# Scores of the first segment from unpermuted weights, and a list scheduler that may hold an engine free

## The chip, the cores and the metric

The kernel runs on one core of a Trainium2 chip. The metric is the device time of that core in microseconds (us); lower is better. Before the change it was 562.31 us, the median of three runs (559.48 to 563.02).

The engines are named as the profile names them: PE (TensorE matmuls), PEld (its weight loads), DVE (VectorE), ACT (ScalarE), POOL (GpSimd), SP (the queue that issues DMAs). "The granted clock" is the share of full TensorE clock that the trace shows; 1.00 is full speed.

## The reference, cut to what matters

Two passes over the same four sublayers: A, B, A, B, each behind a layer norm and with a residual. There are 2048 tokens, 512 channels, 32 heads of 16, all in bf16.

```python
# A: 4 segments of 512 tokens; causal softmax inside a segment, a compressive memory across them
for s in range(4):
    p = softmax(qs @ ks.T * 0.25 + causal_mask)         # per head, 512 x 512
    o = g * (phi(qs) @ M) / (phi(qs) @ z) + (1 - g) * (p @ vs)
    M, z = M + phi(ks).T @ vs, z + phi(ks).sum()
x = x + concat(o) @ wo
# B: linear attention with softmax feature maps
phi_q = concat(softmax(q @ w_phi), softmax(-(q @ w_phi)));  phi_k likewise
o = phi_q @ (phi_k.T @ v) / (phi_q @ phi_k.sum())
x = x + o @ wo_B
```

The work of a pass falls into A's four segments with their score exponentials (40 exponentials of 128x1024 elements for a segment, 160 for a pass), then B's queries and the change to the next pass.

## The kernel before

The program is a graph of operations. Each states the engines that could run it with an assumed duration for each, what it reads and what it writes. A list scheduler, which runs in Python when the kernel is built, simulates this graph and so chooses each engine's order and the buffers; the program then runs in that fixed order on every engine, with semaphores for what crosses engines. So an engine that waits for one operation does not run the next.

The heart of the scheduler takes, for each engine that is free, the most urgent operation that is ready:

```python
def forward(self, prio, pools):
    ...
        for e in ENGS:
            if free[e] > now + 1e-9 or not ready[e]:
                continue
            ...
            while ready[e]:
                pr, i = heapq.heappop(ready[e])
                o = ops[i]
                ...
                if e == "dve" and o.port and free["pool"] > now + 1e-9:
                    held = True          # DVE op that shares a port with POOL: not while POOL is busy
                elif can_alloc(o):       # its buffers are to be had
                    pick = o
                    break
                skipped.append((pr, i))
...
def schedule(self, pools, rounds, off):
    ...
    for r in range(rounds):              # ROUNDS = 5
        mk = self.forward(prio, pools)
        if best is None or mk < best[0]:
            best = (mk, list(prio))
        fin = [o.end for o in self.ops]
        prio = self.backward(fin)
```

In sublayer A, a score matmul takes four heads at once. The keys of eight heads lie in one 128-row tile, two half tiles of 64 rows; the queries are spread to `Q4`, where slot `s` holds only the rows of every fourth head, the rest zero. For this the weights of K and Q are first permuted within each 64 columns, so that the head index is the fastest:

```python
for g in range(NG):
    for k in ("k", "q"):
        for hf in range(2):
            ...                                      # 16 operations, "perm"
            self.g.op({"act": (520, ... activation(dst(), src(), ACT.Copy)),
                       "dve": (285, ... tensor_copy(dst(), src()))},
                      [self.WAraw[k][g // 2]], [R("WP", k, g, hf)], label="perm", port=True)
```

Segments after the first fill `Q4` by DMA into zeroed buffers. The first one, segment (0, 0), has no time for that and writes four whole slots by a multiply with a mask per partition, on ACT or DVE:

```python
self.wproj(ps, 0, self.WA["q"], [R("WP", "q", g, h) for h in range(2)], g, xT, ..., label="Q")
self.evac(lambda: QT.t[:], lambda: ps.t[:, 0:512], 512, [ps[0]], [QT], label="Qev")
for sl in range(nd, 4):                              # nd = 0 in segment (0, 0)
    m = self.S4[:, sl:sl + 1]
    self.g.op({"dve": (262, ... tensor_scalar(Q4.t[:, sl, :], QT.t[:], m, None, op0=ALU.mult)),
               "act": (566, ... activation(Q4.t[:, sl, :], QT.t[:], ACT.Identity, scale=m))},
              [QT, R("S4")], [Q4[sl]], label="Qm", port=True)
...
# the scores of query tile i against key tile j; waits for ALL of Q4
self.mm(... KT.t[:, hf, j*128:(j+1)*128], Q4.t[:, :, i*128:(i+1)*128] ...,
        [512] * 2, [KT[0], KT[1], (Q4, ALLKEYS)], [S], opens=[PT], label="S")
self.act(lambda: PT.t[:], lambda: S.t[:], ACT.Exp, 1024, [S], [PT], scale=0.25, label="exp")
```

There are six `Q4` buffers. Two are zero-filled at the start, after a gate on the normalisation of the fourth token tile:

```python
self.pQ.init[i] = self.g.op({"pool": (1800.0, ... memset(tq[:], 0.0)),
                             "dve": (1070.0, ... memset(tq[:], 0.0))}, [], [], label="zero")
...
gate = self.xnop[3]
for o in ... + list(self.pQ.init.values()):
    o.deps.add(gate)
```

The softmax here doesn't subtract the row's maximum and nothing guards it: scores larger than these inputs give would overflow.

Of the kernel before, what the change touches and what calls it, by code (L numbers as in the profile page):

```python
# [8 lines left out]
ACT = mybir.ActivationFunctionType  # L9
# [11 lines left out]
NG = 4  # L21
# [65 lines left out]

LAT = {"pe": 190, "act": 160, "dve": 130, "pool": 100, "sp": 60}


class Graph:
# [39 lines left out]
    def op(self, ch, reads=(), writes=(), opens=(), kind="c", lat=None, label="", ndma=0, port=False):  # L131
        o = Op()
        o.id = len(self.ops)
        o.ch = ch
        o.deps = set()
        o.succ = []
        o.tiles = []
        o.opens = list(opens)
        o.kind = kind
        o.lat = lat  # L140
        o.label = label
        o.ndma = ndma
        o.need = False
        o.port = port
        o.vc = None
        for r in reads:
            self._touch(o, r, False)
        for w in writes:
            self._touch(o, w, True)
        o.deps.discard(o)  # L150
        self.ops.append(o)
        return o
# [65 lines left out]
    def forward(self, prio, pools):  # L218
        ops = self.ops
        n = len(ops)  # L220
        left = [len(o.deps) for o in ops]
# [26 lines left out]
        now = 0.0  # L248

# [22 lines left out]
        while len(order) < n:  # L272
# [25 lines left out]
# [3 lines that stand above are left out]
                skipped = []  # L301
                pick = None
                held = False
# [3 lines that stand above are left out]
                    if o.eng is not None:  # L307
                        continue
                    if e == "dve" and o.port and free["pool"] > now + 1e-9:
                        held = True  # L310
                    elif can_alloc(o):
                        pick = o
                        break
                    skipped.append((pr, i))
                for x in skipped:
                    heapq.heappush(ready[e], x)
                if pick is None:
                    if held:
                        wake.append(free["pool"])
                    continue  # L320
                o = pick
                for t in o.opens + o.tiles:
                    if t.slot is None:
                        pl = t.pool
                        t.slot = pl.free.pop(0)
                        t.base = pl.base[t.slot]
                        pl.live[t.cls] = pl.live.get(t.cls, 0) + 1
                        pl.opened[t.cls] = pl.opened.get(t.cls, 0) + 1
                o.eng = e
                o.seq = len(order)  # L330
                o.start = now
                dur = o.ch[e][0]
                o.end = now + dur
                free[e] = o.end
                order.append(o)
                lt = o.lat if o.lat is not None else LAT[e]
                heapq.heappush(ev, (o.end + lt, 1, o.id))
                heapq.heappush(ev, (o.end, 2, o.id)) if False else None
                for s in o.succ:
                    left[s.id] -= 1  # L340
                    l2 = 0 if (e == "pe" and "pe" in s.ch and o.kind == "c") else lt
                    rt[s.id] = max(rt[s.id], o.end + l2)
                    if left[s.id] == 0:
                        heapq.heappush(ev, (rt[s.id], 0, s.id))
            nxt = [free[e] for e in ENGS if ready[e] and free[e] > now + 1e-9] + wake
# [11 lines left out]
    def schedule(self, pools, rounds, off):  # L357
        self.link()
        self.log = []
        prio = [float(o.id) for o in self.ops]  # L360
        best = None
        for r in range(rounds):
            try:
                mk = self.forward(prio, pools)
            except RuntimeError as ex:
                if r == 0:
                    raise
                print("round", r, str(ex)[:1200])
                break
            self.log.append(round(mk / 1000, 1))  # L370
            if best is None or mk < best[0]:
                best = (mk, list(prio))
            fin = [o.end for o in self.ops]
            prio = self.backward(fin)
            prio = [p + off.get(o.label, 0.0) for p, o in zip(prio, self.ops)]
        self.model_us = self.forward(best[1], pools) / 1000.0
# [111 lines left out]
class Kernel:  # L488
# [20 lines left out]
    def mm(self, items, cols, reads, writes, opens=(), label=""):  # L509

        dur = sum(max(c / 2.4, 25.0) + 0.5 for c in cols)

        def fn(e):
            ins = None
            for out_ap, lhsT, rhs, st, sp in items():
                ins = e.matmul(out_ap, lhsT, rhs, start=st, stop=sp, tile_position=(basep(lhsT), basep(out_ap)))  # L516
            return ins
        return self.g.op({"pe": (dur, fn)}, reads, writes, opens, label=label)
# [23 lines left out]
    def tpe(self, out_ap, src, reads, writes, opens=(), label=""):  # L542

        ps = self.T(self.pG, "gen")
        pb = lambda: ps.t[:, :].bitcast(BF16)[:, 0:512]

        def fn(e):
            for k in range(4):
                ins = e.transpose(pb()[:, k * 128:(k + 1) * 128], src()[:, k * 128:(k + 1) * 128], self.ident[:])
            return ins  # L550
        self.g.op({"pe": (240.0, fn)}, list(reads) + [self.R("ident")], [ps], opens=opens, label=label + "p")
        self.evac(out_ap, lambda: pb().rearrange("p (a b) -> p a b", a=4), 512, [ps], writes, label=label + "e", fast=True)
# [65 lines left out]
    def setup(self):  # L618
# [4 lines left out]
        def load(pairs, kb, writes, eng="sp", opens=()):  # L623
            dur = 780.0 if eng == "pool" else 470.0
            o = self.g.op({eng: (dur, lambda e: [e.dma_start(o, i) for o, i in pairs()])}, [], writes, opens, kind="d",
                          lat=1300.0 + kb / 0.25, label="load", ndma=1)
# [19 lines left out]
        load(lambda: [(self.beta_sb[:], inp["A_beta"].partition_broadcast(128))], 8, [R("beta")], "pool")  # L646
        self.early = len(self.loads)
# [5 lines left out]
        load(lambda: [(self.wphi_st[:], inp["B_w_phi"].rearrange("(g hl) d j -> (hl d) g j", g=NG))], 16, [R("wphi")])  # L653
# [4 lines left out]
        for g in range(NG):  # L658
# [9 lines left out]
          150, [R("H8")], [R("H8")], eng=P)  # L668
        A8w = self.T(self.pS, "set")
# [7 lines left out]
        v(lambda e: e.tensor_tensor(self.S4[:], self.A8[:, 0:4], self.A8[:, 4:8], ALU.add), 70, [R("A8")], [R("S4")])  # L677
# [13 lines left out]
          [R("gt"), R("A8")], [R("GAm")])  # L691
        v(lambda e: e.tensor_copy(self.GAm[:, :, :, 16], self.A8[:, None, :].to_broadcast([128, NG, 8])), 100,
          [R("A8")], [R("GAm")])
# [29 lines left out]
    def fold_weights(self):  # L723
# [12 lines left out]
        for k in ("k", "q"):  # L736
            raw = self.WBraw[k]
            W = self.T(self.pX, "raw")
            for dt in range(4):
                self.tr(lambda W=W, dt=dt: W.t[:, :, dt * 128:(dt + 1) * 128], lambda raw=raw, dt=dt: raw.t[:, dt, :], [raw], [W[dt]], label="foldT")  # L740
# [72 lines left out]

    def a_proj(self, L, s):
# [5 lines left out]
        for g in range(NG):  # L820
# [5 lines left out]
            self.wproj(ps, 0, self.WA["k"], [R("WP", "k", g, h) for h in range(2)], g, xT, opens=[KT] + ([pk] if pk else []), label="K")  # L826
# [4 lines left out]
            if pk:  # L831
                PK = self.T(self.p1, "PhK")
                self.phi(ps, pk)
                self.tr(lambda PK=PK: PK.t[:].rearrange("p (a b) -> p a b", a=4), lambda pk=pk: pk.t[:], [pk], [PK], label="PhKtr")
# [5 lines left out]
            self.wproj(ps, 0, self.WA["q"], [R("WP", "q", g, h) for h in range(2)], g, xT, opens=[QT] + ([PQ] if PQ else []), label="Q")  # L840
            self.evac(lambda QT=QT: QT.t[:], lambda ps=ps: ps.t[:, 0:512], 512, [ps[0]], [QT], label="Qev")
            nd = 0 if (L, s) in MASKED else 4
            if nd:
                for a in range(0, nd, 2):
                    fn = lambda e, Q4=Q4, QT=QT, a=a: [e.dma_start(Q4.t[sl::4, sl, :], QT.t[sl::4, :]) for sl in (a, a + 1)]
                    self.g.op({"sp": (1300.0, fn)}, [QT], [Q4[("d", a)]], kind="d", lat=1650.0, label="Qx", ndma=2)
            for sl in range(nd, 4):
                m = self.S4[:, sl:sl + 1]
                self.g.op({"dve": (262, lambda e, Q4=Q4, QT=QT, sl=sl, m=m: e.tensor_scalar(Q4.t[:, sl, :], QT.t[:], m, None, op0=ALU.mult)),
                           "act": (566, lambda e, Q4=Q4, QT=QT, sl=sl, m=m: e.activation(Q4.t[:, sl, :], QT.t[:], ACT.Identity, scale=m))},  # L850
                          [QT, R("S4")], [Q4[sl]], label="Qm", port=True)
# [26 lines left out]
    def a_att(self, L, s, i):  # L878
# [9 lines left out]
        for hp in range(2):  # L888
            PV = self.T(self.pG, "pv")
            pvv = lambda PV=PV: PV.t[:, 0:288].rearrange("p (h c) -> p h c", c=18)  # L890
            for gg in range(2):
# [3 lines left out]
                for j in range(i + 1):  # L895
# [5 lines left out]
                        [512] * 2, [KT[0], KT[1], (Q4, ALLKEYS)], [S], opens=[PT], label="S")  # L901
# [209 lines left out]
    def build(self):  # L1111
# [9 lines left out]
        for L in range(2):  # L1121
            if L == 0:
                lnA(0, 0)
                gate = self.xnop[3]
                for o in self.loads[self.early:self.second] + [self.pK.init[k] for k in range(3, 6)] + list(self.pQ.init.values()):
                    o.deps.add(gate)
                self.a_proj(0, 0)
                self.fold_weights()
            for s in range(NSEG):
# [10 lines left out]
                for i in range(4):  # L1140
                    self.a_att(L, s, i)
                    self.ln(s * 4 + i, self.xB[(L, s)], pe=("xB", L, s * 4 + i) in PE_T)
                self.b_keys(L, s, TOK[s])
# [24 lines left out]
ROUNDS = 5  # L1168
OFF = {"warm": 1e6}
N_WARM = 14  # L1170

# [36 lines left out]
```

## Time and profile before

| | before |
|---|---|
| median of 3 runs | 562.31 us |
| profiled span, mean granted clock | 559.1 us, 0.984 |
| first projection / first 1024-wide exp | 11.4 / 20.9 us |
| 20th / 120th / 160th exp | 57.4 / 183.2 / 227.8 us |
| from the 160th exp to the end | 331.3 us |

The exponentials are a good clock for this kernel: the first 160 of them on ACT, 128x1024 each, are exactly the scores of the first pass. I read their start times from the timeline of each trace (to about 0.1 us, because its rows merge operations).

The page of the kernel before: busy times, the span in 40 slices (tenths of busy; the row PEclk is the granted clock), and the share of the engines in the chain of waits that ended last.

```profile
PE 518.8 (93%) x5548; PEld 287.6 (51%) x5548; DVE 450.3 (81%) x992; ACT 495.3 (89%) x652; POOL 220.4 (39%) x395
...
PE   8769899999999999998989998999999899999896
...
PEclk9999999999999999997998999999999999999799
...
PE 53%; DVE 21%; ACT 17%; DMA 4%; POOL 2%; issue 1%; SPq 1%; DVEq 0%
```

No engine limits alone. PE is nearly full in the middle and has room at both ends and around slices 18 to 22 (the change between the passes). The clock dips in slices 18 (250 us), 21 (295 us) and 37 (520 us), counted from 0. The Trainium skill, "TensorE: Matmul & The Clock Gate", section "What's actually happening", says that TensorE has just a half and a full clock, chosen by its recent activity; the trace agrees (below: exactly 0.50 in 525 to 530 us). A stretch at 0.50 is called a half-rate spell here.

The start of the kernel before, from the timeline (start, length, engine, line, operation, out<-in, count, idle time before and what ended it):

```profile
6.93 0.38 DVE L773 TENSOR_SCALAR p<-X,mv,rstd 128x512 bf16<-128x512 bf16 x1
...
9.35 1.80 POOL L716 MEMSET pQ<- 128x2048 bf16 x1 [4.74 <-DVE p L773]
9.81 1.38 DVE L687 TENSOR_SCALAR gt<-gt 128x32 f32<-128x32 f32 x1
11.38 1.04 PE L516 MATMUL G<-pX,WA_q 128*128 128x512 bf16 x4
15.16 1.93 ACT L850 ACTIVATE pQ<-p,S 128x512 bf16<-128x512 bf16 x3
20.87 1.01 ACT L522 ACTIVATE p<-D 128x1024 bf16<-128x1024 f32 x1
```

The first normalisation on DVE is at 6.93 us. POOL fills a `Q4` buffer with zeros from 9.35 us, and a DVE operation on 128x32 elements takes 1.38 us beside it. ACT spends 1.93 us on three mask multiplies before the first exp.

The groups of the operations that the change touches (out<-in, count | busy us, mean ns | idle before):

```profile
L849 DVE TENSOR_SCALAR pQ<-p,S 128x512 bf16<-128x512 bf16 x4 | 1.4, 356 | 0.0
L850 ACT ACTIVATE pQ<-p,S 128x512 bf16<-128x512 bf16 x12 | 8.0, 718 | 0.2 <-DVE p L531 0.2
...
L531 DVE CAST pV<-G 128x512 bf16<-128x512 f32 x11 | 7.5, 688 | 1.3 <-PE G L516 1.1
```

Sixteen mask multiplies cost ACT 8.0 and DVE 1.4 us.

That gap in the timeline of PE:

```profile
521.58 0.95 PE L516 MATMUL G<-Rz,p 128*128 128x16 bf16 x32
524.34 1.03 PE L948 MATMUL G<-ident,p 128*128 128x128 bf16 x8 [1.81 <-DVE p L1101]
...
526.16 1.89 PE L516 MATMUL G<-WB_o,p 128*128 128x512 bf16 x4
```

PE waits 1.81 us for a DVE multiply before it can transpose the first output tile of B (L948).

### The profile page before, as it was taken

Reading aid. Unit: us, or ns where it says so; the run is one execution under the profiler, and the core shown is the slowest. Engines: PE = TensorE matmul, PEld = TensorE weight load, DVE = VectorE, ACT = ScalarE, POOL = GpSimd, SP = SyncE. Lnnn points to the kernel's source line nnn. Section 1 sums busy time; section 2 is a strip of 40 time slices with the busy share of each in tenths; the row PEclk is TensorE's granted clock in tenths of the full one; section 3 lists DMA queues with packets and bytes.
Section 4 is the critical chain, followed back from the end, with each engine's and each line's share of the span. In section 5 each row is a group of like instructions: output and inputs, shape, how many; then the busy total and the mean of one; then the engine's idle time right before and its main releaser. Section 6 shows DMA issues by size and latency. Waiting matters only on the chain.

```text
span 559.1 us, 13700 instructions
## 1 busy us (share of the span) xinstructions
PE 518.8 (93%) x5548; PEld 287.6 (51%) x5548; DVE 450.3 (81%) x992; ACT 495.3 (89%) x652; POOL 220.4 (39%) x395
## 2 busy tenths in 40 slices
PE   8769899999999999998989998999999899999896
PEld 3335445555555656556644453455555456555652
DVE  8979987979787876667999985898777588866784
ACT  6989999999999999887996899979999998987783
POOL 3627536434743653200236452634275364320000
PEclk9999999999999999997998999999999999999799
DMA  6394433112011110000234322120202101000045
GB/s 190 103 189 82 127 78 87 39 39 58 22 29 39 31 29 22 11 1 2 53 70 96 82 70 64 34 57 22 57 20 40 39 21 40 11 20 2 20 131 134
DMA packets 93038, 31.59 MB, mean 57 GB/s; under 512 B 80160, under 2 KB 92976, under 8 KB 92976
## 3 DMA queue, kind: packets, MB, share of 16 engines
q1 hardware_dynamic: 92944, 30.71, 23.3%
q8 instruction: 44, 0.72, 0.5%
q14 instruction: 18, 0.15, 0.1%
q0 software_dynamic: 32, 0.01, 0.0%
HBM read 6.32 MB, written 2.10 MB: 15 GB/s over the span
## 4 chain that ended last, share of the span: by engine, by line
PE 53%; DVE 21%; ACT 17%; DMA 4%; POOL 2%; issue 1%; SPq 1%; DVEq 0%
PE G L516 33%; PE D L516 19%; ACT p L522 16%; DMA p<-p 3%; DVE pK L531 3%; DVE p L1101 2%; DVE stats L752 2%; DVE p L802 1%; DVE p L773 1%; POOL p L906 1%; DVE p L798 1%; DMA wphi_st<-in_B_w_phi_dram 1%; DVE X L966 1%; DVE p L926 1%; DVE p L531 1%
## 5 line engine op out<-in xcount | busy, mean ns | idle before, releaser
L522 ACT ACTIVATE p<-D 128x1024 bf16<-128x1024 f32 x384 | 378.6, 1042 | 32.0 <-PE D L516 25.8
L906 POOL TENSOR_SCALAR_AFFINE_SELECT p<-p 128x512 bf16<-128x512 bf16 x256 | 163.2, 664 | 157.3 <-ACT p L522 156.9
L516 PE MATMUL D<-pQ,pK 128*128 128x512 bf16 x640 | 182.4, 381 | 9.3 <-ACT p L522 6.7
L516 PEld LDWEIGHTS G<-pV,p 128*128 128x128 bf16 x2656 | 84.9, 96 | 37.0 <-POOL p L906 12.3
L516 PE MATMUL G<-pV,p 128*128 128x17 bf16 (+1 forms) x2656 | 89.6, 173 | 7.3 <-POOL p L906 4.2
L516 PEld LDWEIGHTS D<-pQ,pK 128*128 128x128 bf16 x640 | 49.4, 97 | 66.4 <-ACT p L522 32.6
L522 ACT ACTIVATE p<-G 128x512 bf16<-128x512 f32 x112 | 68.7, 626 | 3.9 <-PE G L516 2.7
L760 POOL TENSOR_SCALAR rstd<-mv 128x1 f32<-128x1 f32 x60 | 16.0, 270 | 119.0 <-DVE mv L753 116.2
L1027 DVE TENSOR_REDUCE pS<-p 128x32 f32<-128x512 bf16 x64 | 42.9, 677 | 20.8 <-ACT p L522 20.4
L966 DVE TENSOR_TENSOR X<-X,G 128x512 bf16<-128x512 bf16 x48 | 32.8, 683 | 18.9 <-PE G L516 18.6
L752 DVE BATCH_NORM_STATS2 stats<-X 128x6 f32<-128x512 bf16 x64 | 43.2, 680 | 1.7 <-DMA X<-in_A_x_dram 1.0
L557 DVE RECIPROCAL pS<-G 128x32 f32<-128x32 f32 (+1 forms) x64 | 20.6, 325 | 22.3 <-PE G L516 21.9
L1009 DVE TENSOR_TENSOR pT<-G,pT 128x1024 bf16<-128x1024 f32 x30 | 36.3, 1211 | 1.7 <-PE G L516 1.5
L762 POOL TENSOR_TENSOR rstd<-rstd,mhalf 128x1 f32<-128x1 f32 x60 | 34.7, 583 | 3.4
L516 PE MATMUL G<-pX,WA_k 128*128 128x512 bf16 x128 | 32.7, 379 | 2.8 <-DVE p L926 2.8
L516 PE MATMUL G<-WA_o,p 128*128 128x512 bf16 x128 | 32.9, 379 | 2.3 <-DVE MS L871 1.6
L516 PE MATMUL G<-WB_o,p 128*128 128x512 bf16 x128 | 34.0, 394 | 0.0
L531 DVE CAST pK<-G 64x512 bf16<-64x512 f32 x43 | 29.5, 686 | 5.4 <-PE G L516 4.0
L516 PE MATMUL G<-WA_v,pX 128*128 128x512 bf16 x128 | 32.1, 380 | 1.9 <-POOL rstd L760 1.3
L516 PE MATMUL G<-pX,WA_q 128*128 128x512 bf16 x128 | 32.2, 379 | 1.7 <-DMA pX<-p 1.0
L516 PE MATMUL G<-WB_k,pX 128*128 128x512 bf16 x128 | 32.8, 379 | 0.0
L516 PE MATMUL G<-WB_v,pX 128*128 128x512 bf16 x128 | 32.8, 379 | 0.0
(116 smaller groups left out, 706.9 us busy)
## 6 DMA issues: line engine op xcount, KB each, us to landing
pQ<-p SPq DMA_DIRECT2D x112, 32.0 KB, 1.8
out_dram<-X SPq DMA_DIRECT2D x16, 128.0 KB, 1.8
X<-in_A_x_dram SPq DMA_DIRECT2D x3, 512.0 KB, 4.1
pX<-in_B_wqkv_dram SPq DMA_DIRECT2D x3, 512.0 KB, 4.2
p<-p SPq DMA_TRANSPOSE x80, 2.4
pX<-p SPq DMA_TRANSPOSE x54, 2.4
X<-in_A_x_dram SPq DMA_DIRECT2D x4, 128.0 KB, 2.8
pX<-in_A_wk_dram SPq DMA_DIRECT2D x2, 256.0 KB, 4.1
```

The lines of the kernel that those rows point to most:

```text
L516: ins = e.matmul(out_ap, lhsT, rhs, start=st, stop=sp, tile_position=(basep(lhsT), basep(out_ap)))
L522: return self.g.op({"act": (dur, lambda e: e.activation(out_ap(), in_ap(), func, scale=scale))}, reads, writes, opens, label=label)
L531: "dve": ((340 if fast else n / 0.96 + 65), lambda e: e.tensor_copy(out_ap(), in_ap()))}
L557: return e.reciprocal(o, i)
L752: v(lambda e: e.bn_stats(self.stats[:, t, :], self.X[:, t, :]), 602, [R("X", t)], [R("st", t)], label="bn")
L760: v(lambda e: e.tensor_scalar(rs, self.mv[:, t, 1:2], LN_EPS, None, op0=ALU.add), 170, [R("mv", t)], [R("rstd", t)], eng="pool", label="rstd")
L762: v(lambda e: e.tensor_tensor(rs, rs, self.mhalf[:], ALU.pow), 540, [R("rstd", t), R("mhalf")], [R("rstd", t)], eng="pool", label="rstd")
L906: v(lambda e, pt4=pt4: e.affine_select(pt4(), pt4(), [[0, 4], [1, 128]], ALU.is_ge, 0.0, base=0, channel_multiplier=-1), 560, [PT], [PT[hh ...
L966: self.v(lambda e: e.tensor_tensor(self.X[:, t, :], self.X[:, t, :], ps.t[:, 0:512], ALU.add), 602, [R("X", t), ps[0]], [R("X", t)], label ...
L1009: v(lambda e: e.tensor_tensor(dst(), ps.t[:, None, 0:512].to_broadcast([128, 2, 512]).rearrange("p s (g d h) -> p s g d h", g=NG, h=8), rz ...
L1027: fn = lambda e, sgn=sgn, E=E, Z=Z: e.tensor_reduce(Z.t[:, sgn * 32:(sgn + 1) * 32], E.t[:, sgn * 512:(sgn + 1) * 512].rearrange("p (h d) ...
L1101: v(lambda e, Ns=Ns, Tm=Tm, w=w, shape=shape: e.tensor_tensor(shape(Tm.t[:]), shape(Ns.t[:]), w(), ALU.mult), 600, [Ns, AB[0], AB[1]], [Tm ...
```

## The change

It has two parts. The program part: segment (0, 0) projects K and Q with the raw weights, so the permutation is no longer ahead of the first scores; `Q4` is built by four DVE multiplies with a mask, one for each tile of 128 queries, and the scores of query tile `i` wait only for multiply `i`; the transposes of phi(K) in that segment go to PE; the buffers dirtied by this are zero-filled again later. The scheduler part: before it gives an engine to an operation, it asks whether a more urgent one becomes ready before that operation would end; if so the engine stays free. It tries six settings of this rule and twelve rounds each, models load times by size, and does not start a POOL operation while a port-sharing DVE operation runs.

```diff
+RULES = ((1000.0, 3.0), (1000.0, 2.0), (2000.0, 3.0), (2000.0, 2.0), (500.0, 2.0), (500.0, 3.0))
...
+        def awaited(e, o):
+            q = soon[e]
+            while q and q[0][0] <= now + 1e-9:
+                heapq.heappop(q)
+            end = now + o.ch[e][0]
+            p = prio[o.id] - hold
+            best = None
+            for r, i in q:
+                if r < end and prio[i] < p and end - r > (r - now) * holdk and ops[i].eng is None and can_alloc(ops[i]):
+                    if best is None or r < best:
+                        best = r
+            return best
...
+                    elif e == "pool" and o.kind == "c" and held_port > now + 1e-9:
+                        wake.append(held_port)
                     elif can_alloc(o):
-                        pick = o
-                        break
+                        w = awaited(e, o) if soon[e] else None
+                        if w is None:
+                            pick = o
+                            break
+                        wake.append(w)
...
+        if raw:
+            W = self.WAraw[k]
+            self.mm(... W.t[:, dt, g * 128:(g + 1) * 128], xT.t[:, dt, :] ..., opens=opens, label=label)
...
-            for sl in range(nd, 4):
-                m = self.S4[:, sl:sl + 1]
-                self.g.op({"dve": (262, ... tensor_scalar ...), "act": (566, ... activation ...)}, ...)
+            if raw:
+                for i in range(4):
+                    fn = lambda e, Q4=Q4, QT=QT, i=i: e.tensor_tensor(
+                        Q4.t[:, :, i * 128:(i + 1) * 128], QT.t[:, None, i * 128:(i + 1) * 128].to_broadcast([128, 4, 128]),
+                        self.M4.t[:].rearrange("p (s q) -> p s q", s=4), ALU.mult)
+                    self.v(fn, 335, [QT, self.M4], [Q4[("i", i)]], label="Qm", port=True)
...
-                        [512] * 2, [KT[0], KT[1], (Q4, ALLKEYS)], [S], opens=[PT], label="S")
+                        [512] * 2, [KT[0], KT[1], Q4[("i", i)] if (L, s) in MASKED else (Q4, ALLKEYS)], [S], ...)
...
+                if (L, s) in MASKED:
+                    for Q4 in self.seg[(L, s)]["Q4"]:
+                        self.g.op({"pool": (1800.0, fn), "dve": (1070.0, fn)}, ..., label="clear", port=True)
...
-ROUNDS = 5
+ROUNDS = 12
```

Left out of the diff: PE transposes of phi(K) with a reordering evacuation, an earlier load of B_w_phi on the POOL queue, dependencies that put the permutation behind the first K evacuation, a slightly dearer matmul in the scheduler's model, and two options that are switched off.

## The prediction

> **What bounds the kernel now.** The page gives PE 519, ACT 495, DVE 450 busy of a 559.1 us span. PE's spans overlap, so I count it by pitch: four back-to-back 128x512 matmuls fill 0.86 us in the chain of waits (0.215 each), 32 of 128x17 0.95, eight of 128x136 about 0.5. Over the instruction list that gives an estimate of 510 us of PE work, so PE idles about 49 us: some 18 before 60 us, almost nothing between 80 and 240, the rest around the layer change (260 to 300, where DVE is 91-99% busy) and in the tail after 500. In the middle PE and ACT take turns as the limit (chain of waits: PE 53%, DVE 21%, ACT 17%), so nothing outside those three stretches can gain much.
>
> **The start.** The timeline: first projection at 11.4 us, first score matmul 17.15, first 1024-wide exp 20.9, third 38.0, twentieth about 58. ACT is 90% busy from 10 to 60 us, with 12 mask multiplies (718 ns), 11 weight permutations (630 ns) and evictions among 20 exps. DVE, in order, also stood 2.1 us for the small B_w_phi load (issue to landing 6.3 us, queued behind 512 KB loads); behind it the second-half K evictions and then the third exp waited.
>
> **The change.** Removed: 12 ACT and 4 DVE mask multiplies (8.0 + 1.4 us); permutation from the path to the first scores. Added: 16 DVE multiplies (tensor_tensor 128x512 bf16, median 0.42 us, estimate 7 us in all), four PE transposes with evictions in place of four DMA transposes (1.5 us PE, 2.5 us ACT or DVE), four zero fills of Q4 on POOL (1.8 us each). The new order has 22 small ACT operations ahead of the first exp where there were 33, 41 for 54 ahead of the third, 48 for 59 ahead of the twentieth, 250 for 262 by the last. PE work is +1 us. Adding trace durations along the new order: first projection about 10, first exp about 16, third 31, twentieth 49-51. PE has then also done about 4 us less work, so of the 7-8 us gained on ACT some 5 remain once PE takes over.
>
> **Scheduler.** Every engine's order changes; the instruction mix does not. Holding engines for urgent work, 6x12 candidates and a better port model can trim only the roughly 30 idle us at the layer change and in the tail; in the tail, query projections now stand between the numerator matmuls where PE waited for ACT. Estimate 0 to 8 us, centre 4. The Trainium skill, "SBUF — State Buffer", section "Who interferes with whom", says GpSimd and some VectorE operations exclude each other; the trace agrees (a 128x32 DVE operation took 1380 ns during a POOL fill at 9.4-11.2 us). The new order avoids this only in its model, and real times will drift from it.
>
> **Risk.** The B_w_phi load moves to the POOL queue and its DVE user now stands before the first normalisation in DVE's order. beta's load took 3.6 us from POOL; if this one lands after 7 us it delays everything by the difference (I allow 1-2 us).
>
> **Sum.** 562.3 - 5 (start, net) - 4 (layer change and tail) - about 3 (fewer ACT operations, no B_w_phi stall) = 550; range 541 to 558. Faster by over 2%: 0.53; within: 0.45; slower: 0.02.
>
> **Right if** first exp by 17 us and twentieth by 51; ACT busy about 8 us lower, DVE about 5 higher; middle (80-240) unchanged in pace; PE idle before 60 us down by 5 or more. **Wrong if** the phi load blocks DVE for over 3 us; DVE, more loaded, becomes the limit at 15-60 us; or the new order idles more at the layer change or loses PE clock in the tail (0.83 between 520 and 540 us).

## More of the kernel before

The stretches (from:to, length, then busy time and count of PE, PEld, DVE, ACT, POOL, then granted clock, DMA share and GB/s):

```profile
20.00:60.00 40.00, 31.77 (x291) 16.09 (x290) 35.31 (x88) 36.13 (x50) 19.37 (x34) 1.00 0.64 127
60.00:110.00 50.00, 47.92 (x509) 24.88 (x507) 44.60 (x104) 47.60 (x61) 25.76 (x48) 1.00 0.35 86
...
0.00:227.84 227.84, 210.75 (x2294) 114.50 (x2294) 191.97 (x423) 211.18 (x278) 110.28 (x199) 1.00 0.30 71
227.84:562.00 334.16, 308.05 (x3254) 173.14 (x3254) 258.30 (x569) 284.12 (x376) 110.14 (x196) 0.97 0.19 46
...
520.00:525.00 5.00, 2.50 (x55) 2.24 (x53) 2.78 (x9) 3.95 (x9) 0.00 (x0) 0.87 0.02 3
525.00:530.00 5.00, 5.00 (x55) 3.70 (x53) 3.77 (x9) 2.51 (x5) 0.00 (x0) 0.50 0.18 48
```

From 20 to 110 us DVE is 88 and 89% busy: it has some room, but little. The split at 227.84 us is the 160th exp; 3254 matmuls come after it. The last two rows show a half-rate spell: PE is busy only half of 520 to 525, and in the next 5 us the clock is 0.50 (the spell lasts from 523.66 to 530.49 us).

## The result, and the profile after

The kernel after takes 554.34 us (four runs, 554.09 to 556.35), correct, against 562.14 (the three runs above and a fourth). Its ratio to the kernel before is 0.9878, with a 95% interval of 0.9844 to 0.9913. A ratio here is the mean time of one kernel's fast runs over that of the other's of the same rounds, so not quite the ratio of the medians. A second set of runs gave 552.88 us and 0.9844 (0.9819 to 0.987).

The page of the kernel after, in the same rows:

```profile
PE 510.3 (92%) x5483; PEld 286.7 (52%) x5564; DVE 465.0 (84%) x1009; ACT 489.3 (88%) x640; POOL 224.5 (40%) x400
...
PE   6798889899999999998998899999999999999895
...
PEclk9989989999999999999999899999999999999999
...
PE 51%; DVE 22%; ACT 20%; DMA 4%; issue 2%; POOL 1%; POOLq 0%
```

ACT lost 6.0 us (predicted 8), DVE gained 14.7 (predicted 5). PE's 510.3 is not comparable: 81 of its records are missing (5483 matmuls to 5564 weight loads). The clock dips of slices 18 and 37 are gone in this execution. They are not gone for good: the clock row of the second profile of the same kernel, in the same order (after_again), has them again.

```profile
PEclk9999999999999999998999899999999999999899
```

The start, from the timeline of the kernel after:

```profile
8.65 2.62 DVE L812 TENSOR_SCALAR p<-X,mv,rstd 128x512 bf16<-128x512 bf16 x3
9.12 2.01 POOL L752 MEMSET pQ<- 128x2048 bf16 x1 [2.60 <-DVE p L812]
11.43 0.91 DVE L753 MEMSET pQ<- 128x1024 uint32 x1 [0.16 <-DVE p L812]
12.28 0.40 DVE L812 TENSOR_SCALAR p<-X,mv,rstd 128x512 bf16<-128x512 bf16 x1
13.91 3.61 PE L546 MATMUL G<-pX 128*128 128x512 bf16 x15 [0.78 <-ACT pX L560]
...
19.69 1.02 ACT L552 ACTIVATE p<-D 128x1024 bf16<-128x1024 f32 x1
```

The first exp came 1.2 us earlier, not 4.9 as predicted. Everything ahead of the first projection is later: the first normalisation at 8.65 instead of 6.93 us, three of them stretched to 2.62 us (one alone takes 0.40; the third, begun just after the fill, took 1.98) while POOL fills a `Q4` buffer from 9.12 to 11.13, then a 0.91 us fill on DVE itself ahead of the fourth. The first projection starts at 13.91, predicted about 10. The gate did not keep the fill back: it waits for the normalisation of the fourth token tile, and in the new order (read from the schedule that the build makes) that tile is normalised first, then the second, the first and the third. The Trainium skill, "SBUF — State Buffer", section "Who interferes with whom", says that tensor_scalar and similar DVE operations and GpSimd can shut each other out for a whole instruction; this trace agrees, 2.62 us for three operations of 0.40.

The groups and the stretches of the kernel after:

```profile
L898 DVE TENSOR_TENSOR pQ<-p 128x512 bf16<-128x512 bf16 x16 | 8.0, 522 | 0.0
...
L561 DVE CAST pV<-G 128x512 bf16<-128x512 f32 x17 | 11.5, 684 | 2.1 <-PE G L546 2.0
```

```profile
20.00:60.00 40.00, 34.51 (x318) 17.63 (x321) 39.00 (x89) 36.56 (x51) 21.66 (x40) 0.96 0.52 130
60.00:110.00 50.00, 43.71 (x442) 22.37 (x445) 47.90 (x105) 45.19 (x59) 28.71 (x45) 0.97 0.28 67
...
0.00:229.97 229.97, 209.89 (x2243) 114.48 (x2275) 199.98 (x430) 206.15 (x269) 115.25 (x204) 0.99 0.28 69
229.97:562.00 332.03, 300.40 (x3247) 172.20 (x3293) 265.00 (x580) 283.13 (x373) 109.25 (x196) 0.99 0.20 46
...
520.00:525.00 5.00, 4.18 (x75) 3.58 (x78) 4.89 (x13) 5.00 (x8) 0.00 (x0) 1.00 0.12 26
525.00:530.00 5.00, 4.90 (x29) 2.40 (x28) 4.37 (x12) 4.04 (x8) 0.00 (x0) 1.00 0.51 132
```

Up to the 160th exp ACT has 5.0 us less work and DVE 8.0 us more; from 20 to 60 us DVE is now busy for 39.00 of 40 us, and from 60 to 110 for 47.90 of 50. The mask multiplies are 8.0 us of DVE instead of 1.4, and the scheduler gave DVE six more evacuations of V (11.5 instead of 7.5 us). In 520 to 530 us the clock stays at 1.00 in this execution.

That place in the timeline of PE:

```profile
516.12 0.81 PE L546 MATMUL D<-pX,WB_q 128*128 128x512 bf16 x3
...
520.55 0.62 PE L1005 MATMUL G<-ident,p 128*128 128x128 bf16 x8 [0.97 <-DVE p L1158]
```

Query projections (the first of these rows) now stand between the numerator matmuls, and the wait before the first transpose is 0.97 us instead of 1.81. That does not always save the clock: after_again has the same wait of 0.97 us there, and a half-rate spell from 516.92 to 520.33 us.

Where the time went, by the clock of the exponentials. Every column is one profiled execution; "again" is the second profile of the kernel after.

| start of exp no. | before | after | after, again |
|---|---|---|---|
| 1 | 20.9 | 19.7 | 19.5 |
| 20 | 57.4 | 55.7 | 54.1 |
| 40 | 84.7 | 83.4 | 79.3 |
| 70 | 122.9 | 127.7 | 123.5 |
| 120 | 183.2 | 186.3 | 182.0 |
| 160 | 227.8 | 230.0 | 225.8 |
| end of the span | 559.1 | 554.6 | 552.0 |
| from the 160th exp to the end | 331.3 | 324.6 | 326.3 |
| half-rate spells before the 160th exp, us in all | 0 | 6.8 | 0 |
| half-rate spells after it, us in all | 18.4 | 4.2 | 11.2 |

The early lead of 1 to 5 us is gone by the 70th exp. What the kernel gained, 5 to 7 us, it gained after the 160th, in the change between the passes, the second pass and the tail, where the program part of the change altered no operation. But the last two rows matter here: PE ran at half clock for 18.4 us of that stretch in the profile of before, and for 4.2 and 11.2 us in those of after. If a spell costs half of its length (an estimate, checked below), this alone is 7.1 and 3.6 of the 6.7 and 5.0 us gained there. Up to the 160th exp the columns before and "after, again" have no spell, and there the kernel after is about 2 us ahead. The gain is not because work was moved ahead: the rows of stretches above have 3293 weight loads (one for each matmul) left after the 160th exp, where before had 3254.

### The profile page after: what moved, and what is told of

Same layout as the page of the kernel before. It is cut to its first block, busy times and chain, and to the rows that moved or that the text cites. A ratio compares the mean times of both kernels' runs of the same rounds, so it can differ in the third digit from the quotient of the medians.

```text
span 554.6 us, 13653 instructions
## 1 busy us (share of the span) xinstructions
PE 510.3 (92%) x5483; PEld 286.7 (52%) x5564; DVE 465.0 (84%) x1009; ACT 489.3 (88%) x640; POOL 224.5 (40%) x400
## 4 chain that ended last, share of the span: by engine, by line
PE 51%; DVE 22%; ACT 20%; DMA 4%; issue 2%; POOL 1%; POOLq 0%
PE G L546 32%; PE D L546 19%; ACT p L552 17%; DMA pX<-p 2%; DVE stats L791 2%; DVE pK L561 2%; DVE p L1158 2%; DVE p L561 2%; DVE p L812 1%; DMA p<-p 1%; DVE p L841 1%; DVE p L983 1%; DVE X L1023 1%; DVE p L837 1%; DVE p L1164 1%
## 5 line engine op out<-in xcount | busy, mean ns | idle before, releaser
L546 PE MATMUL D<-pQ,pK 128*128 128x512 bf16 x640 | 182.7, 383 | 8.6 <-ACT p L552 6.9
L799 POOL TENSOR_SCALAR rstd<-mv 128x1 f32<-128x1 f32 x60 | 14.2, 244 | 95.1 <-DVE mv L792 95.0
L561 DVE CAST pK<-G 64x512 bf16<-64x512 f32 x46 | 31.4, 684 | 5.6 <-PE G L546 3.9
L546 PE MATMUL G<-WB_o,p 128*128 128x512 bf16 x123 | 31.6, 379 | 3.1 <-DMA p<-p 2.8
L590 DVE RECIPROCAL pS<-G 128x32 f32<-128x32 f32 (+1 forms) x64 | 20.8, 325 | 13.4 <-PE G L546 13.1
L546 PE MATMUL G<-WB_k,pX 128*128 128x512 bf16 x112 | 29.4, 379 | 2.5 <-DMA pX<-p 1.5
L546 PE MATMUL G<-WB_v,pX 128*128 128x512 bf16 x119 | 30.9, 379 | 0.6
L546 PE MATMUL G<-WA_o,p 128*128 128x512 bf16 x113 | 29.8, 379 | 1.3 <-DVE p L983 0.3
L546 PE MATMUL G<-pX,WA_q 128*128 128x512 bf16 x104 | 27.9, 390 | 2.6 <-ACT p L552 2.1
L546 PE MATMUL G<-pX,WA_k 128*128 128x512 bf16 x102 | 27.2, 386 | 3.4 <-DVE pS L590 2.3
```

Of the source, the lines that this page charges most:

```text
L546: ins = e.matmul(out_ap, lhsT, rhs, start=st, stop=sp, tile_position=(basep(lhsT), basep(out_ap)))
L561: "dve": ((340 if fast else n / 0.96 + 65), lambda e: e.tensor_copy(out_ap(), in_ap()))}
L590: return e.reciprocal(o, i)
L799: v(lambda e: e.tensor_scalar(rs, self.mv[:, t, 1:2], LN_EPS, None, op0=ALU.add), 170, [R("mv", t)], [R("rstd", t)], eng="pool", label="rstd")
```

## The experiments

Twelve runs were made, two of them repeats (after_again and start_again are the kernels after and start); all gave correct results. For all of them:

| kernel | median us (runs) | ratio to before | 95% interval | mean clock |
|---|---|---|---|---|
| sched_only | 557.38 (4) | 0.9927 | 0.9879 to 0.9974 | 0.9885 |
| prog_only | 557.52 (4) | 0.9921 | 0.9872 to 0.9971 | 0.9880 |
| nohold | 565.43 (4) | 1.0062 | 1.0026 to 1.0098 | 0.9872 |
| start | 554.97 (4) | 0.9877 | 0.9832 to 0.9921 | 0.9868 |
| before_fillpe | 559.94 (6) | 0.9951 | 0.9922 to 0.998 | 0.9925 |
| after_again | 552.88 (4) | 0.9844 | 0.9819 to 0.987 | 0.9928 |
| start_again | 550.71 (5) | 0.981 | 0.9785 to 0.9836 | 0.9924 |
| rule0 | 557.99 (4) | 0.9934 | 0.9907 to 0.996 | 0.9900 |
| noport | 554.26 (4) | 0.9877 | 0.9845 to 0.9909 | 0.9925 |
| doubleqm | 558.79 (4) | 0.9953 | 0.9915 to 0.999 | 0.9865 |
| dmafill | 561.42 (6) | 1.0011 | 0.9981 to 1.004 | 0.9830 |
| best | 559.48 (6) | 0.9977 | 0.9948 to 1.0005 | 0.9848 |

The first four share seven runs of the kernel before (median 561.04, mean clock 0.9857), the next four share eleven (561.75, 0.9871), the last four eleven others (560.71, 0.9865). Each of the three groups ran on another chip, so across groups the ratios compare better than the times.

**Reading the clock column.** A spell of length T at half clock lowers the mean by T/2 over the span, and if PE limits throughout it also costs T/2. So span times (1 - clock) is an upper estimate of what the half-rate spells cost a run: 8.0 us for before's seven runs, 4.0 for after_again.

Pairs of profiles with the same order up to the 160th exp show the cost directly. The kernel after had 6.8 us more of half-rate spells there than after_again and reached that exp 4.2 us later; start had 3.4 us more than start_again and came 2.3 us later; before_fillpe, whose edit comes later, had 6.8 us more than before and came 3.0 us later. So in these pairs a spell of 3.4 us cost 1.5 to 2.3 us, about half of its length or somewhat more; the estimate is a fair one rather than a strict upper limit.

### The scheduler alone, and the program alone

sched_only is the program of before with the new scheduler; prog_only is the new program with the old one.

```diff
# sched_only: on the kernel before
-    def forward(self, prio, pools):
+    def forward(self, prio, pools, rule):      # the whole Graph class of after, RULES, load and matmul model
-ROUNDS = 5
+ROUNDS = 12
```

> The program of before (permuted weights first, four scalar masks per group) under the scheduler of after (hold rules, port rule, load model, matmul cost, 6x12 candidates). My theory: the 1.2% come from the new order at the layer change and in the tail, and the program change brings nothing net, so this alone gives 552 to 557 us. Rival: the program change brings the gain and the scheduler nothing, then 560 to 564.

```diff
# prog_only: on the kernel after
-    def forward(self, prio, pools, rule):
+    def forward(self, prio, pools):            # the whole Graph class of before, its matmul model, no load sizes
-ROUNDS = 12
+ROUNDS = 5
```

> The program of after under the scheduler of before (5 rounds, no hold, old costs). My theory: the added VectorE work (16 mask multiplies, zero fills) eats what ScalarE gains, so 559 to 566 us. Rival: the program change is the gain, then 552 to 556.

Measured: each alone is worth 0.7 to 0.8%, about half of the whole 1.2 to 1.6%. A theory that the scheduler gives all and the program nothing is thereby refuted for the total. But where the gain lies is the same in both: the 160th exp came at 232.3 us in sched_only and 233.3 in prog_only, later than before's 227.8, and the rest took 321.0 and 321.8 us instead of 331.3. Half-rate spells account for much of this pattern: before the 160th exp sched_only had 10.2 us of them and prog_only 6.8, before none; after it none and 6.8 us, before 18.4. By half of their length, that is an estimated 5 and 3 us of the delay and 9 and 6 us of the later gain. The rows of the stretches of prog_only, split at its 160th exp:

```profile
0.00:233.27 233.27, 215.20 (x2312) 116.37 (x2313) 199.31 (x433) 208.39 (x272) 117.63 (x205) 0.99 0.27 68
233.27:562.00 328.73, 302.39 (x3254) 171.21 (x3251) 256.89 (x574) 282.30 (x371) 108.84 (x196) 0.99 0.21 46
```

The second row can be held beside before's line by line, since both have 3254 matmuls left and no records are missing. PE takes 302.39 us for them instead of 308.05, 5.7 us less, and idles 321.8 - 302.4 = 19.4 us instead of 331.3 - 308.1 = 23.2, 3.8 us less. The clock is 0.99 instead of 0.97. So in these two profiled executions over half of the difference is PE's own time for the same number of matmuls, which goes with the fewer half-rate spells, and the rest is less waiting. The old scheduler did this with a program whose second pass is the same; only the beginning differs. So prog_only's gain after the 160th exp is no direct saving of the program change: what the changed graph can do there is lead the scheduler to another order. How far that order, and not the luck of one execution, keeps the clock up is not shown by these two profiles.

### The hold rule, its settings and the port rule

nohold switches the new rule off and keeps the rest; rule0 keeps it with the first of its six settings; noport drops the new rule for POOL.

```diff
# nohold
-RULES = ((1000.0, 3.0), (1000.0, 2.0), (2000.0, 3.0), (2000.0, 2.0), (500.0, 2.0), (500.0, 3.0))
+RULES = ((1000.0, 3.0),)
-                        w = awaited(e, o) if soon[e] else None
+                        w = None
```

> After, with only the hold taken out of its scheduler (no engine waits for a nearly ready operation; one candidate series of 12 rounds in place of six). If holding engines free is what pays: 559 to 564 us. If it is only one of several equally good orders: within 3 us of 554.

```diff
# rule0
-RULES = ((1000.0, 3.0), (1000.0, 2.0), (2000.0, 3.0), (2000.0, 2.0), (500.0, 2.0), (500.0, 3.0))
+RULES = ((1000.0, 3.0),)
```

> After with the hold kept but only the first of the six rules as candidate (12 orders in place of 72; the winner of the 72 is another rule's). nohold took 565.4 us. If the hold itself pays: 553 to 558 us. If the wide search over rules is what pays and the hold not: 561 to 566.

```diff
# noport
-                    elif e == "pool" and o.kind == "c" and held_port > now + 1e-9:
+                    elif False:
```

> After with only the port rule taken out of its scheduler (POOL compute no longer waits in the model while a VectorE operation of the excluding kind runs). If modelling the exclusion pays: 557 to 562 us. If it is one of several equally good orders: 551 to 556.

Measured: 565.43 us without holding, 557.99 with holding at one setting, 552.88 to 554.34 with six. So the hold is worth about 1.3% and the choice among six settings another 0.7 to 0.9%. Without it the new program is 0.6% slower than the kernel before. noport's 554.26 lies with the kernel after: the port rule is worth nothing measurable. Three cautions apply. Each switch changes the whole order, so a difference is one draw from a spread of plausible orders of the same operations, here 553 to 565 us. nohold also keeps the other scheduler changes, and with them it is slower than prog_only, which has none of them: without the hold they do harm with this program, in this one order. And in both nohold and rule0 the slow part is the beginning: their 160th exps are at 236.5 and 237.0 us, while the rest took 325.0 and 320.0 us, both shorter than before's 331.3 (rule0's profile has 10.2 us of half-rate spells before its 160th exp, nohold's 3.4, before's none).

### The start: fills behind the normalisations

start keeps the kernel after's order but moves two `Q4` fills and some small DVE set-up operations behind the four normalisations.

```diff
         self.g.schedule(self.pools, ROUNDS, OFF)
+        xn = [self.xnop[t] for t in range(4)]           # the four normalisations of segment (0, 0)
+        for o in self.pQ.init.values():
+            self.later(o, xn)                           # behind them in the order, and dependent on them
+        for o in (RzH, gt1, gt2, A8red, Wbd):           # small set-up operations, where they stood earlier
+            self.later(o, last_xn)
         self.g.emit()
```

> After with its order kept, but for the first 13 us: the two zero fills of Q4 buffers and five small VectorE set-up operations stand behind the four normalisations instead of before or between them. If the exclusion of VectorE by the POOL fill and the set-up work in front are what delayed the first projection (13.9 us against 11.4 before), it starts at 10 to 11 us, the first exp at 16 to 17 us, and the total falls by 2 to 3 us to about 551.5. Rival: VectorE, full from 20 to 105 us, absorbs it and the total stays at 554.

> The same kernel as the run called start. Its four runs went from 552.2 us at clock 0.994 to 556.8 at 0.982, so it may be 2 us faster than after at equal clock and lose that by more clock dips. If so: median 1 to 2 us under after_again, and at clock 0.990 or more always under it. Rival: the earlier start is absorbed, then within 0.7 us of after_again at the same clock.

> The changed kernel unaltered, as the yardstick for the run of start_again on the same chip, and for the relation of time to granted clock over its runs: 554 to 555 us; runs with a mean clock 0.01 lower some 3 us longer.

Measured: the cause of the late start is shown. From the timelines of start:

```profile
6.69 1.02 DVE L812 TENSOR_SCALAR p<-X,mv,rstd 128x512 bf16<-128x512 bf16 x3
7.70 0.41 DVE L812 TENSOR_SCALAR p<-X,mv,rstd 128x512 bf16<-128x512 bf16 x1
8.17 1.80 POOL L752 MEMSET pQ<- 128x2048 bf16 x1 [1.67 <-DVE p L812]
...
10.57 3.61 PE L546 MATMUL G<-pX 128*128 128x512 bf16 x16 [0.78 <-ACT pX L560]
...
17.59 1.02 ACT L552 ACTIVATE p<-D 128x1024 bf16<-128x1024 f32 x1 [0.40 <-PE D L546]
```

All four normalisations are done by 8.11 us (12.68 in the kernel after), the first projection starts at 10.57 and the first exp at 17.59: 3.3 and 2.1 us earlier. Of the 4.6 us by which the normalisations end sooner, 2.0 are there at the first of them, before any fill began, and belong to the set-up operations (the phi multiply among them); the other 2.6 come between the first and the last of them, where the fills stood. At the 20th exp nothing of it is to be seen: 55.2 and 54.8 us in the two profiles of start, 55.7 and 54.1 in those of the kernel after. But the clock was not equal. The clock row of start_again:

```profile
PEclk9889999999999999999999899999999999999999
```

Both profiles of start have two half-rate spells before the 20th exp (17.4 to 20.8 and 27.7 to 31.1 us in start_again), that of the kernel after has one and after_again none. By the cost of a spell found above, these one or two more spells are worth as much as the lead that is missing. So the lead need not have been absorbed by a full DVE; the spells alone can hide it. In the second batch, at equal clock, start took 550.71 us to 552.88 of the kernel after, 2.2 us less. In the first batch it took 554.97, no better than the kernel after, but at a mean clock of 0.9868 to 0.9925; the upper estimate of the clock's cost above gives 7.3 and 4.2 us, a difference of 3.1 that hides the gain. start's own runs show the same: 552.2 us at 0.994, 556.82 at 0.982. So about the whole of the 2.1 us by which the first exp is earlier arrives in the total at equal clock.

### DVE as the limit: every mask multiply twice

doubleqm is start with each of the 16 mask multiplies done twice, first into scratch. The idea was that DVE absorbs the start's gain; then adding to DVE must delay the exponentials nearly in full.

```diff
-                    fn = lambda ...: e.tensor_tensor(Q4.t[:, :, i*128:(i+1)*128], ..., ALU.mult)
+                    fn = lambda ...: [e.tensor_tensor(d, ..., ALU.mult)
+                                      for d in (self.scr[:, i % 2], Q4.t[:, :, i*128:(i+1)*128])][-1]
```

> The kernel start with every one of the 16 mask multiplies of the first segment done twice (the first copy into a scratch buffer; the result stays right), order otherwise kept: about 7 us more VectorE work between 13 and 38 us. If VectorE is what limits the stretch from 20 to 110 us, the twentieth exp comes 4 to 7 us later than in start (53.8) and the total grows by 3 to 7 us over start's 551 to 553. Rival (ScalarE or TensorE limits): twentieth exp within 2 us, total within 1.5 us.

Measured: the 20th exp is at 58.0 us (54.8 in start_again), the 120th at 188.4 (182.7), so some 3 us are lost by the 20th and 5.7 by the 120th. The added multiplies take 7.4 us in its trace. Half-rate spells do not explain the delay: doubleqm has 3.4 us of them before its 20th exp, start_again 6.8. The total is 558.79 us to 550.71 of start_again; 3.3 us of that difference are within the upper estimate for the clock (7.5 and 4.2 us), which leaves about 5 to 8. The stretch from 20 to 60 us, of start_again:

```profile
20.00:60.00 40.00, 34.64 (x323) 17.87 (x326) 37.66 (x87) 35.94 (x49) 20.86 (x38) 0.95 0.54 131
```

And of doubleqm:

```profile
20.00:60.00 40.00, 31.44 (x290) 15.57 (x288) 39.68 (x94) 33.19 (x46) 21.28 (x37) 0.96 0.49 125
```

With DVE at 39.68 of 40 us, PE did 290 matmuls instead of 323 and ACT 46 operations instead of 49. More DVE work delays the others here. That is direct evidence that DVE limits this stretch. It does not show that DVE swallowed the lead of start, which the half-rate spells can account for.

### Two gaps of PE filled

before_fillpe is the kernel before, its order kept, with eight dummy matmuls of 128x512 in front of the first output transpose of B in each pass, where PE had waited 1.81 us.

```diff
+    for L in range(2):
+        first = first "otp" operation of pass L          # the transposes of L948
+        # 8 x matmul(first's PSUM tile, onesb, onesb broadcast); the tile is overwritten by first itself
+        self.fillpe(first, first.tiles[-1], 8)
```

> Before with its order kept, plus eight dummy 128x512 matmuls (1.7 us at full clock) in each of the two gaps in which PE waits for the first weighted numerator (253.3 to 255.1 us and 522.5 to 524.3 us in the trace of before). If PE's idling there is what lowers its granted clock right after (0.70 at 250-260, 0.68 at 520-530), those two dips vanish or shrink and the mean clock rises from about 0.985 to 0.990 or more, and the time falls by 1 to 2.5 us. Rival: the clock dips have another cause (then they stay) or cost nothing (then the time stays within 0.7 us of before).

Measured: ratio 0.9951, at most 0.998: faster by some 0.5%, in spite of 1.9 us of added PE work in either place. The rows of the stretches of before_fillpe around the second gap:

```profile
520.00:525.00 5.00, 4.20 (x88) 3.23 (x87) 3.22 (x12) 4.54 (x8) 0.00 (x0) 1.00 0.01 3
525.00:530.00 5.00, 4.33 (x59) 2.83 (x59) 4.32 (x11) 3.25 (x8) 0.00 (x0) 1.00 0.00 0
```

and from the timeline of its PE:

```profile
524.69 1.89 PE L1127 MATMUL G<-onesb 128*128 128x512 bf16 x8
526.65 0.62 PE L948 MATMUL G<-ident,p 128*128 128x128 bf16 x8
```

The clock stays at 1.00 where it had fallen to 0.50, and the eight transposes take 0.62 us instead of 1.03. So the idling of PE around a gap of under 2 us brings the half-rate spell on here: in the 3.41 us before the spell of the kernel before (520.25 to 523.66) PE was busy for 1.59 us, and no single wait in it was longer than 1.81. Filling the gap pays although the filling does nothing. Part of the first gap's spell remains (0.66 in 255 to 260 us, 0.50 before). The mean clock over all runs rises from 0.9871 to 0.9925. This is a third to two fifths of what the kernel after gains.

### Zero fills by DMA, and the best parts together

dmafill is start with all six `Q4` fills taken from POOL and DVE and given to the DMA queue, to free DVE. best adds five dummy matmuls in each of the two gaps.

```diff
# dmafill
-            {"pool": (1800.0, ... memset(tq[:], 0.0)), "dve": (1070.0, ... memset(tq[:], 0.0))}
+            {"sp": (650.0, ... dma_start(tq[:], zeros[:, None, :].to_broadcast([128, 4, 512])))}
# best: dmafill, and
+            self.fillpe(first, first.tiles[-1], 5)
```

> The kernel start with all six zero fills of Q4 buffers done by DMA from a small zero tile instead of POOL (four, 1.8 to 2.0 us each, which shut VectorE out) and VectorE (two, 0.91 us). If the fills cost VectorE time in its full stretch (4 to 7 us with the exclusion), the hundredth exp comes 2 to 4 us earlier than in start and the total falls by 1 to 3 us to about 550. Rival: the fills' DMAs hold up the query copies and transposes behind them on the SP queue, then no gain or up to 3 us loss.

> dmafill plus five dummy 128x512 matmuls in each of the two gaps before the first weighted numerator (as in before_fillpe). If the clock dips at 250 and 520 us go: mean clock 0.993 or more and 0.5 to 1.5 us under dmafill. Otherwise the same as dmafill within 0.7 us.

Measured: both failed. dmafill took 561.42 us, 10.7 us more than start_again (on another chip; by the ratios, 2.0%), of which the lower mean clock is some 5.4 by the estimate above; best took 559.48. In the order in which SP issues, the fills stand ahead of loads and transposes: a transpose issued at 85.45 us, just behind a fill, landed 5.6 us later, where the median in start_again is 2.4. From the waits of dmafill between 14 and 110 us (engine, line, waited for: total us, times, longest):

```profile
PE G L546 <- DMA p<-p: 8.6, 2, 4.4
...
ACT p L552 <- PE G L546: 6.5, 1, 6.5
```

PE waited 8.6 us for two DMA transposes, and ACT 6.5 us behind it. The 120th exp is at 192.8 us, 10 us later than in start_again. best was 0.3% faster than dmafill in the same rounds, by medians, which is within the spread. The fills should stay on the engines. best is not the best version; start is, at 550.71 us, 1.9% under the kernel before (unclear by the 2% line: the interval reaches 0.9836) and 0.4% under the kernel after in the same rounds.

## Why the prediction was right or wrong

The measured 554.34 us lies in the range (541 to 558); the point, 550, was 4 us low, and the likelier class in the prediction, faster by over 2%, did not come about. The sum was 5 + 4 + 3 us; measured were 8. That the total fell into the range is in part luck: of the 8 us expected from the start and from ACT, about 2 were there by the 160th exp (before and after_again, both without half-rate spells until then), and much of what came later in the profiles goes with half-rate spells, which the sum had no term for.

- **"PE has then also done about 4 us less work, so of the 7-8 us gained on ACT some 5 remain once PE takes over."** This step failed. ACT did lose its mask multiplies (495.3 to 489.3 us busy), but DVE took over, not PE. The mis-sized term is DVE's added work: "about 5 higher" was 14.7. The multiply takes 522 ns on average, not the 0.42 us of a similar operation elsewhere (8.0 us for 16, not 7, and only 1.4 us left DVE in exchange), and the new order gave DVE six more V evacuations, 4.0 us; together these are 10.6 of the 14.7, and the 48 normalisations took 24.2 us of DVE instead of 22.0. I had counted the instructions that the diff adds and trusted that the scheduler would leave the others where they were. A DVE that was 88% busy from 20 to 60 us had no room for that. It became 98% busy, and doubleqm shows that it limits there. The prediction had named this as a risk but gave it no number.
- **"First projection about 10, first exp about 16, third 31, twentieth 49-51."** Measured 13.9, 19.7, 33.0, 55.7. The normalisations started later and ran beside a POOL fill; start shows that moving the fills and the set-up operations restores 10.6 and 17.6. Its twentieth, 55.2, is no test, because two half-rate spells come before it. PE was busy for 48.6 of the first 60 us in after_again and for 47.3 in before, so its idling fell by some 1.3 us there, not by 5 or more. I had read the new order on each engine but not asked which of its fills would run beside which normalisation, though I had quoted the rule and the 1380 ns that should have made me ask. The "about 3 us" for fewer ACT operations did not show either: by the 160th exp the kernel after is 2.1 us late in its first profile, with 6.8 us of half-rate spells, and 2.1 us early in the second, without any.
- **"Estimate 0 to 8 us, centre 4" from the change of passes and the tail.** Right in place, and 5.0 to 6.7 us came from after the 160th exp; but by the estimate above 3.6 of the 5.0 and all of the 6.7 go with the longer half-rate spells of before's profile, and not with the trimmed idling that the prediction counted on. The mechanism that I had named, query projections between the numerator matmuls, is there (the wait is 0.97 instead of 1.81 us), and before_fillpe shows what such a gap costs: the half-rate spell behind it more than the gap.
- **"The phi load blocks DVE for over 3 us."** It did not: the load landed 3.9 us after its issue at 2.2 us, and its user on DVE ran at 8.05 us without waiting. It did take 0.68 us of DVE just ahead of the first normalisation.
- **Middle unchanged in pace.** Right: from the 120th to the 160th exp 44.6 us before, 43.7 after.

What stays open is why every one of the reordered kernels is faster than before after the 160th exp, by 5 to 11 us (before_fillpe, with before's own order, by 2.8). Half-rate spells are a large part of it in these profiles, since before's has 18.4 us of them there and no other more than 11.2. Over all runs, by the upper estimate, the clock is worth up to 3.3 of the 8.9 us between before and after_again in the same batch, so about half of the gain or more has another source. In the comparison with prog_only PE also idles 3.8 us less, and I did not find one feature of before's order that causes it. That some of it is luck among orders is plausible, since the spread of orders is as large as the gain, but it was not tested by drawing many of them.

## What to carry to other kernels

Before counting a saving on one engine, read how full the engine is that receives the work, in that very stretch: here 6 us less on ACT went with 15 us more on a DVE that was 88% busy, and the lead of up to 5 us at the 40th exp was gone by the 70th. When a scheduler chooses the order, a change of a few operations reorders everything, so compare stretches of equal work (here, from the 160th exp to the end) before crediting the change with the difference, and expect the order alone to be worth a per cent either way. Look at the granted clock beside every time, and before comparing two profiles list the half-rate spells of each: two executions of one kernel differed by 4.2 us at the same exp through two of them. Look also at PE gaps of 1 to 2 us: filling two of them with useless matmuls gained half a per cent.

## What the Trainium skill lacked or had wrong

- "TensorE: Matmul & The Clock Gate", section "HAM oscillation — how this bites in real kernels": it states the rule "no PE-idle gaps >~3.4µs". Here no gap around 522 us was longer than 1.81 us, yet with PE busy for 1.59 of 3.41 us a spell of 6.83 us at clock 0.50 began; with eight dummy matmuls in the gap the clock stayed at 1.00. As a rule for such gaps it is too lenient. Further down the page does name frequent short idles as a second cause, but gives no length for them.
- The same page, section "What's actually happening", puts the penalty of the first ramp below 1% of a typical span and calls it variable from run to run. No run here measures that ramp by itself. What the section has no figure for is spells in the middle of a kernel: one kernel (start) ran 552.2 us at a mean clock of 0.994 and 556.82 at 0.982, 0.8%, as large as most of the differences studied here, so two runs must be compared at equal clock.
- "SBUF — State Buffer", section "Who interferes with whom", says who blocks whom and quotes two slowdowns, but none for a fill beside a row of short operations: three normalisations of 0.40 us each took 2.62 us beside one POOL fill of 2.01 us.
- No page that I read has a figure for what a large fill by DMA costs the transfers behind it on its queue: with six fills of a 128x2048 bf16 buffer moved to the SP queue, one transpose behind a fill took 5.6 us to land instead of 2.4, PE waited up to 4.4 us for transposes, and the kernel took 10.7 us more (up to 5.4 of them by its lower clock).
